# A fused attention and expert kernel: PSUM banks in strict turn, early weights decoded in another order, part of the routing moved to GpSimd

## The chip, the core and the metric

The kernel runs on one core of a Trainium2 chip. Five engines work side by side, each through its own queue of instructions in order: TensorE (PE, with its weight loads as PEld) multiplies matrices into PSUM; VectorE (DVE), ScalarE (ACT) and GpSimd (POOL) work elementwise; SyncE (SP) issues most transfers. They wait for each other through semaphores. The metric is the device time of one execution in microseconds; the time of a kernel is the median of its runs.

## What is computed

Attention with capped scores, a gated product of two linear maps, and a layer of eight experts that sends each token to one of them. All values are float32.

```python
def _attn_ref(q, k, v, cap):                     # 2 x 12 heads, 448 tokens, 64 wide
    scores = cap * np.tanh(scale * q @ k.T / cap)
    attn = softmax(scores)                       # with 1e-9 added to the sum
    return attn @ v

def _moe_ref(x, w_a, w_b, w_out):                # 896 x 768, inner width 1536
    return (x @ w_a) * (x @ w_b) @ w_out

def _moe2_ref(x, w_gate, w1, w2):                # 8 experts, 768 -> 1024 -> 768
    logits = x @ w_gate
    expert_idx = np.argmax(logits, axis=1)
    gate_w = softmax(logits)[expert_idx]
    out[mask_e] = gate_w * (np.maximum(x[mask_e] @ w1[e], 0) @ w2[e])
```

(`q @ k.T` and the softmaxes are abbreviated here; the weights of the product come as 64-bit floats and are decoded on the chip.)

## The kernel before

The instructions stand in each queue in the order in which the code below writes them; no scheduler moves them.

**Attention** (`attention`, L150) walks over 12 pairs of heads. For each pair n, TensorE makes the scores of four chunks of keys (`ps_s`, L100), ScalarE takes Tanh (L104) and for two chunks together Exp (L106) into `e`, and GpSimd adds the two chunks of each half into `u` (L112, the *fold*). VectorE adds the two halves (L115). TensorE multiplies `e` with v (`ps_o`, L125) and, from `u` and a matrix of ones, makes the sums (`ps_sm`, L131). VectorE then takes the reciprocal `r` (L139), multiplies `xf` (L140) and splits that into a high and a low part `xh`, `xl` (L142, L143). One iteration holds the scores of pair n, the product with v of pair n-1, and the sums and the norm of pair n-2. Ahead of the scores VectorE scales the queries of each pair by 1/(8 cap) (`attn_prep`, L91), two pairs ahead. Transfers of `qk` and `v` run through SP's queue, between those of the first raw weights.

In the first two iterations VectorE also decodes the first column blocks of `w_a` and `w_b` (`b1_decode`, L260; `early` puts all of it on VectorE): raw words to float (L253 to L258), high part `wh` (L242), low part `wl` (L268). Before all this `attn_flag` (L59) tests whether |cap| exceeds 40; only then does another path for attention run (`attn_general`).

**PSUM.** Four one-bank tiles carry the tag `p1`, and two two-bank tiles the tag `s2`. A new tile of a tag takes a bank that is free by the pool's record, and its first writer waits for the last reader of the tile before.

**The product** (`b1_products`, L274) computes both linear maps over 12 column blocks, each matmul in three parts (high by high, high by low, low by high). **The output** (`b2_tile`, L492) then makes seven tiles of 128 tokens in `ps_y` (tag `s2`, so two at a time); after each, ScalarE copies the tile to a `row` in SBUF (L508), and `gate_steps` (L545) finds the expert of each token: for tiles 0, 1, 2, 4 and 5 eight VectorE products with a gate column each (`jk`, L569), for tiles 3 and 6 matmuls. `route_steps` (L606) ranks the tokens of a group by expert (tiles 0 to 3 are group 0, tiles 4 to 6 group 1): `ranks`, `totals`, `sizes`, `bases`, `blocks`, `past`, `meta`, `ranked`, `places`, `onehot`, `lists`. The steps of group 1, with what is left of the gate, are a list `todo`; `pop` (L471) writes the next of them into the code of an expert block, seven times in a block.

**The experts** (`d_block`, L845): block s gathers 128 rows by an indirect transfer on GpSimd, loads the weights of its expert, splits them into high parts (ScalarE, L794) and low parts (VectorE, L797: `w1l`, `w2l`), and runs two layers. Between the layers TensorE transposes each half of the hidden values; ScalarE writes `hth`, VectorE the low part `htl` (L823), and the second layer (L842, L843) takes both. Ten blocks are executed here.

Of the kernel before, what the change touches and what calls it, by code (L numbers as in the profile page):

```python
# [23 lines left out]
CP, NCH = 112, 4  # L24
# [13 lines left out]
class Kernel:  # L38
# [20 lines left out]
    def attn_flag(self):  # L59

        nc, cp, cap = self.nc, self.const, self.cap1
        ab = cp.tile([1, 2], F32, name="capabs")
        big = cp.tile([1, 1], I32, name="big")
        nc.vector.tensor_scalar(ab[:, 0:1], cap, -1.0, None, op0=ALU.mult)
        nc.vector.tensor_tensor(ab[:, 1:2], cap, ab[:, 0:1], op=ALU.max)
        nc.vector.tensor_scalar(big, ab[:, 1:2], CAP_DIRECT, None, op0=ALU.is_gt)
        self.bigv = nc.values_load(big[0:1, 0:1], min_val=0, max_val=1)
# [25 lines left out]
    def attn_scores(self, n, c):  # L93

        nc = self.nc
        qk = self.ld[n][0]
        ps = self.ps.tile([128, 2, 512], F32, name="ps_s", tag="s2", bufs=2)
        for j in range(2):
            r = slice(64 * j, 64 * j + 64)
            nc.tensor.matmul(ps[:CP, j, :S], qk[r, 1, c * CP : (c + 1) * CP], qk[r, 0], start=True, stop=True)  # L100
        if c == 0:
            self.e[n] = self.awork.tile([CP, NCH, 2, S], F32, name="e", bufs=2)
        e = self.e[n]
        nc.scalar.activation(e[:, c], ps[:CP, :, :S], AF.Tanh)  # L104
        if c % 2:
            nc.scalar.activation(e[:, c - 1 : c + 1], e[:, c - 1 : c + 1], AF.Exp, scale=self.cap[:CP])  # L106
# [43 lines left out]
    def attention(self):  # L150
# [3 lines left out]
        for n in range(npair):  # L154
            self.attn_load(n + RING - 1)
            self.attn_scores(n, 0)
            self.attn_scores(n, 1)
            if n > 0:
                self.attn_pv(n - 1, 0, 1)
            self.attn_fold(n, 0)  # L160
            if n > 1:
                self.attn_sums(n - 2)
                self.attn_norm(n - 2)
            self.attn_prep(n + 2)
            if n < 2:
                self.b1_decode(0, n, early=True)
            self.attn_scores(n, 2)
            self.attn_scores(n, 3)
            if n > 0:
                self.attn_pv(n - 1, 2, 3)  # L170
            self.attn_fold(n, 1)
        self.attn_pv(npair - 1, 0, 1)
# [4 lines left out]
    def attn_general(self):  # L177
# [10 lines left out]
        with self.tc.If(self.bigv > 0, label="general"):  # L188
            sc = self.attn_scale()
            for b, hp in ((b, hp) for b in range(B) for hp in range(NP)):  # L190
# [3 lines left out]
                po = self.p1("ps_go")  # L194
                for j in range(2):
                    rows = slice(64 * j, 64 * j + 64)
                    et = [tile_of(f"ge{i}", [CP, 2, S]) for i in range(2)]
                    for c in range(NCH):
                        cs = slice(c * CP, (c + 1) * CP)
                        ps, pt = self.p1("ps_gs"), self.p1("ps_gt")  # L200
# [105 lines left out]
    def run(self):  # L306
# [24 lines left out]
        self.raw, self.w = {}, {}  # L331
# [17 lines left out]
        self.attn_prep(0)  # L349
# [161 lines left out]
    def p1(self, name, dt=F32):  # L511
        return self.ps.tile([128, 512], dt, name=name, tag="p1", bufs=4)
# [32 lines left out]
    def gate_steps(self, i, xr, py):  # L545
# [19 lines left out]
        def product(e):  # L565
            if "lg" not in st:
# [3 lines left out]
                jk, py[:, :DM], 1.0, self.wgb[e], op0=ALU.mult, op1=ALU.mult, accum_out=st["lg"][:, e : e + 1],  # L570
# [35 lines left out]
    def route_steps(self, g):  # L606
        nc, tw, n = self.nc, self.tw, GT[g]
        st = {}

        def T(shape, name, dt=F32):  # L610
# [12 lines left out]
        def totals():  # L623
            rk, tt = st["rk"], st["tt"]
            for t in range(1, n):
                nc.vector.tensor_tensor(rk[:, t], rk[:, t], tt[:, t - 1], op=ALU.add)
                nc.vector.tensor_tensor(tt[:, t], tt[:, t], tt[:, t - 1], op=ALU.add)
# [54 lines left out]
        def ranked():  # L682
# [3 lines left out]
            nc.vector.tensor_tensor(pr[:, 0, :n], rk[:, :n], self.oh[g], op=ALU.mult)  # L686
            nc.vector.tensor_tensor(
# [16 lines left out]
        def onehot(t):  # L704
            rp = st["rp"]
            nc.vector.tensor_scalar(st["a"][:, t], self.iota, rp[:, 0, t : t + 1], None, op0=ALU.is_equal)
            tk = GT[0] * g + t
            nc.vector.tensor_scalar(
# [136 lines left out]
    def d_block(self, s):  # L845
# [18 lines left out]
        self.pop()  # L864
        self.d_split2(6)
        ha = self.d_ht(0, ha)
        self.pop()
# [17 lines left out]
        if more:  # L885
            self.d_xt(s + 1, 1)()
            self.d_split1(4, 5)
        self.d_w2(hb, 6, 7)
# [62 lines left out]
```

## Time and profile before

| | |
|---|---|
| median of 3 runs (lowest to highest) | 589.39 us (588.01 to 590.59) |
| the profiled execution | 586.97 us |
| its span, first to last instruction | 585.2 us |
| mean granted TensorE clock | 0.988 |
| busy: PE, DVE, ACT, POOL | 554.0, 478.9, 335.6, 92.4 us |

Attention fills the stretch up to about 112 us, the product the one up to 289 and the output up to 384 us; the expert blocks follow. TensorE is busy for 95% of the span. A time in a row of the timeline is that of the start, then the duration; in square brackets stands how long the engine was idle just before and what released it. A wait of TensorE is what a shorter time can be won from, as far as nothing else becomes late in its place. The granted clock is 1.00 at 2.4 GHz and 0.50 at 1.2 GHz.

### The profile page before, as it was taken

To read this page: it belongs to the slowest core of one execution; us is meant where nothing else is said; L and a number is where in the kernel's file an instruction comes from. 1 tells how busy PE (TensorE), PEld (TensorE's weight loads), DVE (VectorE), ACT (ScalarE), POOL (GpSimd) and SP (SyncE) were. 2 spreads that over 40 slices of the span, in tenths; PEclk is the share of its full clock that TensorE was granted. 3 is DMA by queue.
4 is the path that set the end of the run, shared out by engine and by line. 5 is a ranking of instruction groups with operands and counts; after the bars stand their busy time and mean duration, and the time that the engine had idled before them with its cause. 6 is when DMAs were issued, how large, how long until landed. Compare 5 with 4: busy or idle time off the path is not lost. (4 is left out here: it accounts for less than half of the span.)

```text
span 585.2 us, 8722 instructions
## 1 busy us (share of the span) xinstructions
PE 554.0 (95%) x2835; PEld 432.4 (74%) x2835; DVE 478.9 (82%) x757; ACT 335.6 (57%) x423; POOL 92.4 (16%) x64
## 2 busy tenths in 40 slices
PE   4799999899999999999999999899989999999994
PEld 1222333499999999999988888778868888888883
DVE  1699999988887777777578848887998998988984
ACT  3958998424333333333451121476877789888893
POOL 0645555300000000000000000501020011110110
PEclk9989999999999999999999999999999999999998
DMA  5972200045545444410061006686110499200110
GB/s 175 336 227 95 63 1 0 1 165 203 173 164 176 153 171 158 172 47 39 2 201 43 28 27 238 207 333 228 57 54 28 170 345 387 104 15 28 56 55 34
DMA packets 21344, 75.51 MB, mean 129 GB/s; under 512 B 3553, under 2 KB 3553, under 8 KB 21282
## 3 DMA queue, kind: packets, MB, share of 16 engines
q1 hardware_dynamic: 19458, 67.68, 33.0%
q0 software_dynamic: 1680, 7.10, 3.6%
q8 instruction: 27, 0.44, 0.3%
q14 instruction: 35, 0.29, 0.1%
q10 hardware_dynamic: 144, 0.00, 0.0%
HBM read 118.80 MB, written 6.70 MB: 214 GB/s over the span
## 5 line engine op out<-in xcount | busy, mean ns | idle before, releaser
L284 PE MATMUL ps_ab<-xh,wh 128*128 128x448 f32 x288 | 105.1, 365 | 0.0
L286 PE MATMUL ps_ab<-xh,wl 128*128 128x448 f32 x288 | 105.0, 364 | 0.0
L285 PE MATMUL ps_ab<-xl,wh 128*128 128x448 f32 x288 | 105.0, 364 | 0.0
L797 DVE TENSOR_TENSOR w1l<-r,w1h 128x1024 fp32r<-128x1024 f32 x63 | 74.2, 1220 | 8.8 <-ACT w1h L794 8.8
L797 DVE TENSOR_TENSOR w2l<-r,w2h 128x768 fp32r<-128x768 f32 x80 | 72.4, 952 | 2.8 <-ACT w2h L794 1.9
L244 ACT ACTIVATE wh<-wf 128x768 fp32r<-128x768 f32 x22 | 18.6, 846 | 86.4 <-DVE wf L258 86.4
L794 ACT ACTIVATE w1h<-r 128x1024 fp32r<-128x1024 f32 x66 | 66.2, 1052 | 2.1 <-PE ps_y L500 2.1
L499 PE MATMUL ps_y<-woh,hs 128*128 128x512 f32 x168 | 64.6, 404 | 2.1 <-DVE jk L569 2.1
L112 POOL TENSOR_TENSOR u<-e 112x896 f32<-112x896 f32 x24 | 54.7, 2279 | 54.1 <-ACT e L106 51.4
L794 ACT ACTIVATE w2h<-r 128x768 fp32r<-128x768 f32 x80 | 61.8, 838 | 0.0
L284 PEld LDWEIGHTS ps_ab<-xh,wh 128*128 128x128 f32 x288 | 54.1, 188 | 5.6 <-issue 1.4
L285 PEld LDWEIGHTS ps_ab<-xl,wh 128*128 128x128 f32 x288 | 54.1, 188 | 4.1
L286 PEld LDWEIGHTS ps_ab<-xh,wl 128*128 128x128 f32 x288 | 54.0, 187 | 4.1
L100 PE MATMUL ps_s<-qk 64*112 64x448 f32 x192 | 46.7, 611 | 9.3 <-DVE qk L91 8.6
L104 ACT ACTIVATE e<-ps_s 112x896 f32<-112x896 f32 x48 | 41.4, 909 | 21.7 <-PE ps_s L100 21.6
L500 PE MATMUL ps_y<-woh,hs 128*128 128x256 f32 x168 | 47.1, 281 | 0.0
L100 PEld LDWEIGHTS ps_s<-qk 64*112 64x112 f32 x192 | 16.4, 187 | 38.4 <-issue 14.3
L106 ACT ACTIVATE e<-e,cap 112x1792 f32<-112x1792 f32 x24 | 42.9, 1789 | 0.8
L125 PE MATMUL ps_o<-e,v 112*64 112x448 f32 x192 | 41.3, 552 | 0.0
L569 DVE SCALAR_TENSOR_TENSOR jk<-ps_y,wgb 128x768 f32<-128x768 f32 x40 | 38.3, 957 | 3.6 <-PE ps_ix L716 1.3
L832 PE MATMUL ps_w<-w1h,xht 128*128 128x512 f32 x120 | 40.3, 403 | 0.0
L832 PE MATMUL ps_w<-w1l,xht 128*128 128x512 f32 x120 | 39.6, 397 | 0.0
(154 smaller groups left out, 1069.2 us busy)
## 6 DMA issues: line engine op xcount, KB each, us to landing
r<-w SPq DMA_DIRECT2D x66, 512.0 KB
r<-w SPq DMA_DIRECT2D x88, 384.0 KB
raw_wa<-wa SPq DMA_DIRECT2D x12, 768.0 KB
raw_wb<-wb SPq DMA_DIRECT2D x12, 768.0 KB
raw_wo<-wo SPq DMA_DIRECT2D x12, 768.0 KB
qk<-qk SPq DMA_DIRECT2D x12, 448.0 KB
wgb<-wgt SPq DMA_DIRECT2D x8, 384.0 KB
x1g<-row SPq DMA_DIRECT2D x7, 386.0 KB
```

The lines of the kernel that those rows point to most:

```text
L100: nc.tensor.matmul(ps[:CP, j, :S], qk[r, 1, c * CP : (c + 1) * CP], qk[r, 0], start=True, stop=True)
L104: nc.scalar.activation(e[:, c], ps[:CP, :, :S], AF.Tanh)
L106: nc.scalar.activation(e[:, c - 1 : c + 1], e[:, c - 1 : c + 1], AF.Exp, scale=self.cap[:CP])
L112: self.nc.gpsimd.tensor_tensor(u, e[:, 2 * half], e[:, 2 * half + 1], op=ALU.add)
L284: nc.tensor.matmul(o, wh[:, k], xh, start=k == 0, stop=False)
L285: nc.tensor.matmul(o, wh[:, k], xl, start=False, stop=False)
L286: nc.tensor.matmul(o, wl[:, k], xh, start=False, stop=k == KC - 1)
L499: nc.tensor.matmul(ps[:, 0:512], hs[:, hh, k], w[:, 0:512], start=st, stop=sp)
L500: nc.tensor.matmul(ps[:, 512:768], hs[:, hh, k], w[:, 512:768], start=st, stop=sp)
L794: self.nc.scalar.activation(hl[0], raw, AF.Copy)
L797: (engine or self.nc.vector).tensor_tensor(hl[1], raw, self.f(hl[0]), op=ALU.subtract)
L832: self.nc.tensor.matmul(self.pw1[half], a[:, k], w[:, cs], start=k == 0 and i == 0, stop=k == KC - 1 and i == 2)
```

## The change

1. `p1` gives its four banks in strict turn (a tag for each bank) in place of one tag with four buffers.
2. Pair 0 isn't scaled by VectorE; its Tanh takes the scale. The decode of the first block of `w_a` stands ahead of the scaling of pair 2, that of `w_b` at the end of iteration 0, behind the fold.
3. `attn_flag` is one instruction: cap times cap, compared with 40 squared.
4. The `jk` products of tile 4 read the row copy in SBUF, not `ps_y`.
5. For group 1, `totals`, the products of `ranked` and the one-hots run on GpSimd.
6. In blocks 0 to 3, `htl` of the first half stands ahead of the split of `w2` chunk 6. The pop between the chunks 5 and 6 is dropped, and one is added behind the last split of `w1`, so the steps of group 1 move by a place or so.

```diff
-        ab = cp.tile([1, 2], F32, name="capabs")
-        nc.vector.tensor_scalar(ab[:, 0:1], cap, -1.0, None, op0=ALU.mult)
-        nc.vector.tensor_tensor(ab[:, 1:2], cap, ab[:, 0:1], op=ALU.max)
-        nc.vector.tensor_scalar(big, ab[:, 1:2], CAP_DIRECT, None, op0=ALU.is_gt)
+        nc.vector.tensor_scalar(big, cap, cap, CAP_DIRECT**2, op0=ALU.mult, op1=ALU.is_gt)
...
-        nc.scalar.activation(e[:, c], ps[:CP, :, :S], AF.Tanh)
+        nc.scalar.activation(e[:, c], ps[:CP, :, :S], AF.Tanh, **({} if n else {"scale": self.sc[:CP]}))
...
+            if n == 0:
+                self.b1_decode(0, 0, early=True)
             self.attn_prep(n + 2)
-            if n < 2:
-                self.b1_decode(0, n, early=True)
...
             self.attn_fold(n, 1)
+            if n == 0:
+                self.b1_decode(0, 1, early=True)
...
-        self.attn_prep(0)
         self.attn_prep(1)
...
-    def p1(self, name, dt=F32):
-        return self.ps.tile([128, 512], dt, name=name, tag="p1", bufs=4)
+    def p1(self, name, dt=F32, at=None):
+        if at is None:
+            at = self.turn = (self.turn + 1) % 4
+        return self.ps.tile([128, 512], dt, name=name, tag=f"p1{at}")
...
-                jk, py[:, :DM], 1.0, self.wgb[e], op0=ALU.mult, op1=ALU.mult, accum_out=st["lg"][:, e : e + 1],
+                jk, xr[:, :DM] if i == 4 else py[:, :DM], 1.0, self.wgb[e], op0=ALU.mult, op1=ALU.mult, accum_out=st["lg"][:, e : e + 1],
...
+        eng = nc.gpsimd if g else nc.vector
...
-                nc.vector.tensor_tensor(rk[:, t], rk[:, t], tt[:, t - 1], op=ALU.add)
+                eng.tensor_tensor(rk[:, t], rk[:, t], tt[:, t - 1], op=ALU.add)
...
         self.d_split2(4, 5)
-        self.pop()
-        self.d_split2(6)
+        routing = s < GT[0]
+        if not routing:
+            self.d_split2(6)
         ha = self.d_ht(0, ha)
+        if routing:
+            self.d_split2(6)
         self.pop()
...
             self.d_split1(4, 5)
+        self.pop()
         self.d_w2(hb, 6, 7)
```

The same replacement of `nc.vector` by `eng` stands in `ranked` (two products) and `onehot` (two instructions for each of three tiles). The other path for attention only gets fixed banks.

On VectorE, the opening of attention before (the first row stands for the scaling of pairs 0, 1 and 2; `raw_wa`, `raw_wb` are the raw weights, `u` the fold's add):

```order
L91 TENSOR_SCALAR qk<-qk,sc 128x448 x3
L253 TENSOR_SCALAR wf<-raw_wa 128x768
L256 TENSOR_SCALAR dc<-raw_wa 128x768
L257 SCALAR_TENSOR_TENSOR wf<-wf,k_78,dc 128x768
L258 SCALAR_TENSOR_TENSOR wf<-raw_wa,ksign,wf 128x768
L242 CAST wh<-wf 128x768
L268 TENSOR_TENSOR wl<-wf,wh 128x768
L115 TENSOR_TENSOR u_2333<-u_2333,u_2311 112x896
L91 TENSOR_SCALAR qk<-qk,sc 128x448
L253 TENSOR_SCALAR wf<-raw_wb 128x768
```

And after, from the scaling of pair 1:

```order
L88 TENSOR_SCALAR qk<-qk,sc 128x448
L252 TENSOR_SCALAR wf<-raw_wa 128x768
L255 TENSOR_SCALAR dc<-raw_wa 128x768
L256 SCALAR_TENSOR_TENSOR wf<-wf,k_78,dc 128x768
L257 SCALAR_TENSOR_TENSOR wf<-raw_wa,ksign,wf 128x768
L241 CAST wh<-wf 128x768
L267 TENSOR_TENSOR wl<-wf,wh 128x768
L88 TENSOR_SCALAR qk<-qk,sc 128x448
L112 TENSOR_TENSOR u_2329<-u_2329,u_2307 112x896
L252 TENSOR_SCALAR wf<-raw_wb 128x768
L255 TENSOR_SCALAR dc<-raw_wb 128x768
```

The first decode now follows the scaling of pair 1 at once; that of pair 2 stands behind it, and the second decode ahead of the scaling of pair 3.

On VectorE, block 2 before, around `htl` of the first half (`rt_ri`, `rt_rp` belong to the places, `rt_a`, `rt_b` to the one-hots; `w2l` from `r_6` is that of chunk 6):

```order
L797 TENSOR_TENSOR w2l_5228<-r_5_5162,w2h_5227 128x768
L695 CAST rt_ri<-rt_rr 128x3
L696 TENSOR_SCALAR rt_ri<-rt_ri 128x3
L697 TENSOR_SCALAR rt_ri<-rt_ri 128x3
L698 CAST rt_rp<-rt_ri 128x2x3
L699 TENSOR_TENSOR rt_rp<-rt_rp,rt_rr 128x3
L797 TENSOR_TENSOR w2l_5230<-r_6_5163,w2h_5229 128x768
L823 TENSOR_TENSOR htl<-ps_ht,hth 128x512
L706 TENSOR_SCALAR rt_a<-iota,rt_rp 128x128
L708 TENSOR_SCALAR rt_b<-iota,rt_rp,tok 128x22
```

And after:

```order
L800 TENSOR_TENSOR w2l_5224<-r_5_5158,w2h_5223 128x768
L826 TENSOR_TENSOR htl<-ps_ht,hth 128x512
L800 TENSOR_TENSOR w2l_5226<-r_6_5159,w2h_5225 128x768
L698 CAST rt_ri<-rt_rr 128x3
L699 TENSOR_SCALAR rt_ri<-rt_ri 128x3
L700 TENSOR_SCALAR rt_ri<-rt_ri 128x3
L701 CAST rt_rp<-rt_ri 128x2x3
L702 TENSOR_TENSOR rt_rp<-rt_rp,rt_rr 128x3
L800 TENSOR_TENSOR w2l_5228<-r_7_5160,w2h_5227 128x768
L800 TENSOR_TENSOR w1l_5206<-r_0_4339,w1h_5205 128x1024
```

`htl` has moved ahead of the places and of chunk 6, and the one-hots are gone from VectorE's queue.

On GpSimd after, the blocks 1 to 3 (before, only the gathers `xg` and the stores `out` stood there):

```order
L765 DMA xg_5019<-x1g,idc_131 128x772
L629 TENSOR_TENSOR rt_rk<-rt_rk,rt_tt 128x8
L630 TENSOR_TENSOR rt_tt<-rt_tt 128x8
L629 TENSOR_TENSOR rt_rk<-rt_rk,rt_tt 128x8
L630 TENSOR_TENSOR rt_tt<-rt_tt 128x8
L899 DMA out<-y,idx_129 896x768
L765 DMA xg_5285<-x1g,idc_131 128x772
L689 TENSOR_TENSOR rt_pr<-rt_rk,oh_128 128x24
L690 TENSOR_TENSOR rt_pr<-oh_128,rt_base 128x24
L709 TENSOR_SCALAR rt_a<-iota,rt_rp 128x128
L711 TENSOR_SCALAR rt_b<-iota,rt_rp,tok 128x22
L709 TENSOR_SCALAR rt_a<-iota,rt_rp 128x128
```

Totals, products and one-hots stand there in that order, between and behind the transfers.

## Rows read from the trace of the kernel before

**Rows 1.** TensorE's waits, 0 to 112 us: total, times, longest

```profile
PE ps_sm L131 <- DVE u L115: 3.9, 1, 3.9
PE ps_sm L131 <- DVE r L139: 2.7, 6, 1.7
```

**Rows 2.** TensorE's waits, 382 to 425 us and 425 to 460 us

```profile
PE ps_w L842 <- DVE htl L823: 0.9, 1, 0.9
...
PE ps_w L842 <- DVE htl L823: 3.0, 2, 2.8
```

**Rows 3.** Stretches: length, busy PE, PEld, DVE, ACT, POOL, then clock, DMA share, GB/s

```profile
45.00:60.00 15.00, 14.72 (x72) 4.59 (x68) 14.79 (x13) 13.22 (x13) 9.04 (x4) 1.00 0.28 93
...
112.00:340.00 228.00, 228.00 (x1165) 207.02 (x1162) 180.53 (x324) 77.23 (x111) 0.40 (x5) 1.00 0.35 122
...
367.00:371.00 4.00, 1.94 (x12) 1.46 (x11) 3.79 (x14) 0.30 (x2) 1.24 (x2) 1.00 0.33 99
...
438.00:441.00 3.00, 3.00 (x12) 2.61 (x12) 3.00 (x7) 0.93 (x2) 0.00 (x0) 0.50 0.00 0
```

**Rows 4.** Timeline, opening of attention, VectorE: start, duration, engine, line, operation, tiles

```profile
2.79 0.15 DVE L65 TENSOR_TENSOR capabs<-cap,capabs 1x1 f32<-1x1 f32 x1
...
14.17 0.45 DVE L91 TENSOR_SCALAR qk<-qk,sc 128x448 f32<-128x448 f32 x1 [5.63 <-DMA qk<-qk]
...
19.04 1.52 DVE L91 TENSOR_SCALAR qk<-qk,sc 128x448 f32<-128x448 f32 x1 [4.41 <-DMA qk<-qk]
...
21.53 1.02 DVE L257 SCALAR_TENSOR_TENSOR wf<-wf,k,dc 128x768 int32<-128x768 int32 x1
...
22.59 2.73 DVE L258 SCALAR_TENSOR_TENSOR wf<-raw_wa,ksign,wf 128x768 int32<-128x768 int32 x1
...
37.34 2.95 DVE L139 RECIPROCAL r<-ps_sm 128x448 f32<-128x448 f32 x1
```

**Rows 5.** Timeline, steady attention, VectorE and GpSimd

```profile
45.14 2.94 DVE L139 RECIPROCAL r<-ps_sm 128x448 f32<-128x448 f32 x1
...
49.36 2.42 POOL L112 TENSOR_TENSOR u<-e 112x896 f32<-112x896 f32 x1 [1.34 <-ACT e L106]
49.75 2.28 DVE L91 TENSOR_SCALAR qk<-qk,sc 128x448 f32<-128x448 f32 x1
...
51.95 1.08 DVE L115 TENSOR_TENSOR u<-u,u 112x896 f32<-112x896 f32 x1
...
52.95 2.94 DVE L139 RECIPROCAL r<-ps_sm 128x448 f32<-128x448 f32 x1
...
53.72 2.10 POOL L112 TENSOR_TENSOR u<-e 112x896 f32<-112x896 f32 x1 [1.94 <-ACT e L106]
```

**Rows 6.** Timeline, end of the output stage

```profile
355.20 0.81 ACT L508 ACTIVATE row<-ps_y 128x768 f32<-128x768 f32 x1 [4.50 <-issue]
...
370.22 0.48 PE L499 MATMUL ps_y<-woh,hs 128*128 128x512 f32 x1 [2.06 <-DVE jk L569]
...
382.17 0.69 DVE L785 TENSOR_TENSOR xlt<-ps_xd,xht 128x512 fp32r<-128x512 f32 x1 [2.38 <-ACT xht L784]
```

**Rows 7.** Timeline, expert blocks 0 to 2

```profile
400.89 0.17 DVE L577 COPY lg<-ps_lg 128x8 f32<-128x8 f32 x1 [2.10 <-PE ps_lg L575]
...
415.64 0.19 PEld L842 LDWEIGHTS ps_w<-w2h,htl 128*128 128x128 f32 x1 [0.43 <-DVE htl L823]
...
416.63 0.16 DVE L627 TENSOR_TENSOR rt_tt<-rt_tt 128x8 f32<-128x8 f32 x1
...
434.44 0.16 DVE L695 CAST rt_ri<-rt_rr 128x3 int32<-128x3 f32 x1
...
435.36 0.96 DVE L797 TENSOR_TENSOR w2l<-r,w2h 128x768 fp32r<-128x768 f32 x1
...
436.97 0.51 PE L842 MATMUL ps_w<-w2h,htl 128*128 128x512 f32 x1 [2.76 <-DVE htl L823]
...
448.89 1.27 POOL L891 DMA_INDIRECT out<-y,idx  x1 [19.41 <-ACT y L890]
```

More of the change, by code (lines that the diff above doesn't have):

```diff
@@ L193, in attn_general @@
                 nc.sync.dma_start(v, self.io["v"][b, hp])
-                po = self.p1("ps_go")
+                po = self.p1("ps_go", at=0)
                 for j in range(2):
@@ L199, in attn_general @@
                         cs = slice(c * CP, (c + 1) * CP)
-                        ps, pt = self.p1("ps_gs"), self.p1("ps_gt")
+                        ps, pt = self.p1("ps_gs", at=1 + c % 2), self.p1("ps_gt", at=3)
                         nc.tensor.matmul(ps[:CP, :S], qk[rows, 0, cs], qk[rows, 1], start=True, stop=True)
@@ L330, in run @@
         self.gx = tc.dram_tile((B, 2, 128, KC, S), F32, name="gx")
-        self.raw, self.w = {}, {}
+        self.raw, self.w, self.turn = {}, {}, 0
         self.xg, self.xt = {}, {}
@@ L625, in totals @@
             for t in range(1, n):
-                nc.vector.tensor_tensor(rk[:, t], rk[:, t], tt[:, t - 1], op=ALU.add)
-                nc.vector.tensor_tensor(tt[:, t], tt[:, t], tt[:, t - 1], op=ALU.add)
+                eng.tensor_tensor(rk[:, t], rk[:, t], tt[:, t - 1], op=ALU.add)
+                eng.tensor_tensor(tt[:, t], tt[:, t], tt[:, t - 1], op=ALU.add)
         def sizes():
@@ L685, in ranked @@
             pr, rr = T([2, 4, NE], "pr"), T([2, 4], "rr")
-            nc.vector.tensor_tensor(pr[:, 0, :n], rk[:, :n], self.oh[g], op=ALU.mult)
-            nc.vector.tensor_tensor(
+            eng.tensor_tensor(pr[:, 0, :n], rk[:, :n], self.oh[g], op=ALU.mult)
+            eng.tensor_tensor(
                 pr[:, 1, :n], self.oh[g], base.unsqueeze(1).to_broadcast([128, n, NE]), op=ALU.mult
@@ L705, in onehot @@
             rp = st["rp"]
-            nc.vector.tensor_scalar(st["a"][:, t], self.iota, rp[:, 0, t : t + 1], None, op0=ALU.is_equal)
+            eng.tensor_scalar(st["a"][:, t], self.iota, rp[:, 0, t : t + 1], None, op0=ALU.is_equal)
             tk = GT[0] * g + t
-            nc.vector.tensor_scalar(
+            eng.tensor_scalar(
                 st["b"][:, t], self.iota[:, :NSP], rp[:, 1, t : t + 1], self.tok[:, tk : tk + 1],
```

## The prediction

> **What bounds the kernel now.** I read first the list of TensorE's waits, stretch by stretch, because only an engine that never waits sets the time. From 112 to 340 us the list is empty and TensorE is busy for 228.00 of 228.00 us [rows 3]; from 460 us to the end it is empty again. What the change could give there is nothing, and it touches nothing there. So the whole effect has to come out of three places, and I read each in the timeline. (A) Attention: TensorE waits 3.9 us once for a folded sum `u` and 2.7 us in six places for the reciprocal `r`, both made by VectorE [rows 1]. VectorE is busy for 14.79 of 15 us while attention runs steadily [rows 3], so there it is VectorE that sets the pace: one pair costs it 52.95 - 45.14 = 7.81 us [rows 5]. (B) The output product: its last tile waits 2.06 us for the products `jk` of tile 4 [rows 6]. (C) The expert blocks 0 to 3: waits for `htl` of 0.9 us in block 0 and 3.0 us in two places later [rows 2], of which 2.76 us stand at 436.97 in block 2 [rows 7]; a last one, of 0.43 us in block 1 at 415.64, is too short for the list [rows 7].
>
> **A: the opening and the banks.** Before, VectorE sits idle for 4.41 us until pair 2's queries land at 19.04, and only then decodes the first weights [rows 4]. After, the same work stands between the scaling of pair 1 and the first reciprocal, but the first decode goes ahead of that wait, and the second goes behind the first fold. The weights of that decode were asked for ahead of pair 1's queries, which are there at 14.17, so the decode can start then. That closes 4.41 us. The flag loses two instructions of some 0.17 us each from start to start (one is shown at 2.79), which stand before the branch and so before those loads: 0.35 us. Sum 4.76.
>
> What it costs shows in the same rows. A VectorE instruction that reads only SBUF and meets a GpSimd fold takes about 1.7 to 1.8 us longer: 2.73 against 1.02 for two like steps of the decode [rows 4], and 2.28 against 0.45 for the same scaling, with a fold at 49.36 beside it [rows 5, 4]. The Trainium skill states why ("SBUF — State Buffer", "Who interferes with whom": VectorE with two SBUF inputs, or in a two-port mode, and a GpSimd instruction that reads SBUF hold one port pair by turns, for a whole instruction each); the rows agree, though it names no price. The fold of pair 0's first half met an idle VectorE; now it meets a decode: +1.75. The next one cost only 1.07 (scaling 1.52 against 0.45 [rows 4]); now it meets a longer instruction: +0.7. So 4.76 - 2.45 = 2.3 us; I take the first reciprocal 2.0 us earlier than 37.34 [rows 4]. If one fold more collides before it, 0.3 is left.
>
> Pair 0's scaling moves into its Tanh: 0.45 us (the price of the one at 14.17 [rows 4]) go from the way to the first matmul, but TensorE is not late there, so I cost it at nothing; the cover is the wait for pair 1's queries.
>
> The strict turn of the four banks moves a wait, no instruction. Before, the sums of pair n took the bank of the sums of pair n-1, so TensorE stood until that reciprocal was read (six waits, 2.7 us [rows 1]). After, the output of pair n takes the bank of pair n-2's output and waits for VectorE's `xf`, the instruction behind the reciprocal, one iteration later; pv, sums and the next scores are queued behind it. In the steady part VectorE is full, so TensorE only waits elsewhere: nothing gained, and nothing lost as long as VectorE's 7.81 us hold. What the opening gives is then carried to the end of attention: **A = -2.0**. The bound on the good side is 4.41, if the folds collide no more than before; on the bad side I take one pair's collision, +1.5, for new ones in the steady part.
>
> **B: tile 4's gate from SBUF.** The wait of 2.06 us at 370.22 is for a bank that eight `jk` instructions read; after, they read the row copy, which ScalarE has made at 355.20 (0.81 us), and the bank is free twelve us too early to matter [rows 6]. What is late next: the first expert input is split by VectorE at 382.17, after 2.38 us of idle time [rows 6], so VectorE can come forward by most of this. Two SBUF inputs may cost each `jk` up to 0.13 us, which is how far the decode's like step (1.02 [rows 4]) lies from theirs, 1 us in all; that eats idle time first. **B = -2.0**, between -2.06 and -1.0.
>
> **C: routing of the second group.** In blocks 0 to 3 `htl` now stands ahead of `w2l` of chunk 6, worth 0.96 us [rows 7]. Block 0's wait of 0.9 goes, and block 1's 0.43. In block 2 VectorE has no pause between 410 and 441 us, so what leaves its queue ahead of `htl` counts in full: `w2l` 0.96; the five place instructions, from 434.44 to 435.36, 0.92, now behind `htl`; the four running totals at 0.14 each from start to start (one at 416.63), 0.55; two products, 0.25 [rows 7]. That is 2.7 us. VectorE also starts the blocks about 1.5 us earlier (B), and the 2.10 us that it lost at 400.89 waiting for a transpose [rows 7] may go, since that step is popped later. TensorE comes 2.06 + 0.9 + 0.43 = 3.4 us earlier to the spot. So 436.9 - 2.7 - 1.5 - (0 to 2.1) against 434.2 - 3.4: a wait of 0 to 1.9, where it was 2.76; I take 1.2. After the 2.76 us the granted clock was 0.50 for all of 438 to 441 [rows 3], its lower level (1.2 GHz); 3.0 us at half speed lose 1.5, and I add 0.2 for the edges: 1.7. After the 2.06 us at 370.22 it stayed at 1.00 [rows 3]. So a wait of 1.2 should not lower it. Behind that, `w2l` 6 and the places now stand ahead of the second half's `htl`, and TensorE comes to it early and fast: a new wait of 0.6 to 1.6, taken as 1.0. Sum: -0.9 - 0.4 - 1.5 - 1.7 + 1.0 = **C = -3.5**, between -1.5 (below) and -5.5 (no wait in block 2).
>
> GpSimd gets twelve small instructions. Its queue in these blocks holds only a gather and a store each, with 19.41 us idle ahead of the store at 448.89 [rows 7]. The totals stand behind block 2's gather, the products behind block 3's; one-hots come last, and TensorE asks for them only in block 3. No row prices them on GpSimd; a fold of 896 columns takes 2.42 [rows 5], so by its length one of 128 columns takes 0.35 or so, and the small ones not under VectorE's 0.14. I take 0.3, 3.6 us in all, well inside the idle time; both ends leave it there.
>
> **Sum.** -2.0 - 2.0 - 3.5 = -7.5. The profiled execution takes 586.97 us for a span of 585.2, and lies 2.4 below the median of 589.39; I expect an execution like it at 579.5 and a median of **581.9**.
>
> **The rivals.**
> - *GpSimd gives it back.* Each moved instruction reads SBUF, and VectorE does little but subtractions of two SBUF inputs there. If each of the twelve holds VectorE for its 0.3 us, 3.6 come back, more than totals and products (0.8) and the six one-hots saved; the clock falls again in block 2 and C is -1.5: 583.9. For it speak the collisions in A; against it, that only the six of totals and products stand ahead of the critical `htl`. The Trainium skill speaks against such moves ("Perfetto Trace Analysis", "Optimizing Scalar/DVE Operations": the two engines share a read port, so offloading between them might not help). By it the sum would be that of this rival; the trace of before has no small GpSimd instruction among the blocks, and so leaves it open. 0.20.
> - *The opening gives nothing.* A sixth collision, or weights that land later than I read, leave A between 0 and -0.3; with B and C as above -5.5 to -5.8, and with a worse tail -4: about 584. 0.15.
> - *The opening gives all.* If folds slip between PSUM-fed instructions, A is -4.4: 579.5. 0.13.
> - *Slower: the folds meet the fold's add in every pair.* GpSimd's first fold of a pair starts at 53.72, 1.77 us after the add at 51.95 has started [rows 5]. TensorE no longer stands for the reciprocal, so scores, Exp and that fold can run ahead. From the point where the fold starts before the add, each pair loses 2.28 - 0.45 = 1.83 [rows 5, 4], on top of the collision that it has. Five pairs outweigh the -7.5; nine give +16.5 and 598.4. Against it: `e` has two buffers, and VectorE's add is what lets GpSimd go on. 0.08.
> - *The turn changes nothing.* The matmuls keep their order, so if `xf` comes as late for TensorE as the reciprocal did, only the place of the wait differs. That is inside my forecast, since I give the turn nothing.
>
> **Chances.** The forecast as it stands 0.42; with the rivals above 0.98; 0.02 for what I don't see. A measurement of this kernel can tell about 0.5%, 2.9 us, from no change, so faster means under 586.4: the forecast, the upper opening, most of the GpSimd rival and of the weak opening, together 0.80. Within 0.5%: the rest of these two, 0.12. Slower 0.08. The range runs from 577 (the good bounds of A and half of C's) to 587 (two of the weak cases together); it leaves out the slower rival and the ends.
>
> **What would show it.** First reciprocal near 35.3, and the product stage some 2 us earlier; no wait for `jk`; `htl` of blocks 0 and 1 without a wait; in block 2 a wait under 2 us and a clock of 1.00 behind it. Wrong would be: scaling and fold's add both over 2 us in each pair; VectorE's `w1l` and `w2l` lengthened beside GpSimd's one-hots; a clock of 0.50 near 435.

## The result, and the profile after

The changed kernel takes 579.72 us (median of 4 runs, 578.74 to 580.21), the kernel before 589.53 us beside it. The ratio is 0.9833, with a 95% interval of 0.9808 to 0.9859: 9.8 us less, where 7.5 were forecast. The profiled execution has a span of 577.0 us, 8.2 less than the 585.2 of before. The sign, the size and the three places were forecast rightly; of the three terms, two came out much as worked out and one, the opening of attention, came by another way. The ratios leave out executions over 1.5% above the fastest of the same kernel, which below concerns two of the twelve of e1_turn, at 922.08 and 1112.86 us.

TensorE's waits of the changed kernel (engine, line, waited for, total, times, longest), from 0 to 112 us and from 425 to 460 us; from 112 to 425 us the list is empty:

```profile
PE ps_s L97 <- PEq L187: 8.1, 1, 8.1
PE ps_s L97 <- issue: 4.1, 2, 3.8
PE ps_s L97 <- DVE qk L88: 2.9, 1, 2.9
PE ps_o L122 <- ACT e L103: 1.3, 1, 1.3
...
PE ps_w L845 <- DVE htl L826: 1.4, 2, 1.1
```

The first line is the time up to the first matmul, 8.6 us in the kernel before. The waits for `u` and `r` [rows 1] are gone. In their place stand 2.9 us for the scaled queries of pair 1, 3.8 us that the profile gives no releaser ("issue"), and 1.3 us for `e` near the end of attention. The 3.8 us end when VectorE has scaled the queries of pair 3, as the rows below show (34.36 and 2.26 us). The wait for `jk` is gone, and of those for `htl` [rows 2] 1.4 us are left, 1.1 in one place.

Where the 8.2 us come from is read from the first instructions of each stage, in us from the start of the span:

| first instruction | before | after | gain so far |
|---|---|---|---|
| product stage (`ps_ab`) | 112.75 | 111.24 | 1.5 |
| output stage (`ps_y`) | 288.68 | 287.17 | 1.5 |
| experts (`ps_w`) | 383.64 | 379.24 | 4.4 |
| store of block 1 | 425.94 | 420.37 | 5.6 |
| store of block 2 | 448.89 | 440.67 | 8.2 |
| store of block 9 | 577.88 | 569.82 | 8.1 |

The opening of attention after, VectorE and one row of TensorE (start, duration, engine, line, operation, tiles; in brackets the idle time before and its releaser):

```profile
7.75 0.16 DVE L69 RECIPROCAL sc<-cap 128x1 f32<-128x1 f32 x1 [4.96 <-DVEq L187]
...
14.67 2.02 DVE L88 TENSOR_SCALAR qk<-qk,sc 128x448 f32<-128x448 f32 x1 [6.57 <-DMA qk<-qk]
...
18.71 2.73 DVE L257 SCALAR_TENSOR_TENSOR wf<-raw_wa,ksign,wf 128x768 int32<-128x768 int32 x1
...
23.02 2.29 DVE L88 TENSOR_SCALAR qk<-qk,sc 128x448 f32<-128x448 f32 x1
...
27.28 2.74 DVE L256 SCALAR_TENSOR_TENSOR wf<-wf,k,dc 128x768 int32<-128x768 int32 x1
...
31.11 2.34 DVE L241 CAST wh<-wf 128x768 fp32r<-128x768 f32 x1
...
34.36 2.26 DVE L88 TENSOR_SCALAR qk<-qk,sc 128x448 f32<-128x448 f32 x1
...
36.73 3.07 PE L97 MATMUL ps_s<-qk 64*112 64x448 f32 x8 [3.80 <-issue]
37.55 2.94 DVE L136 RECIPROCAL r<-ps_sm 128x448 f32<-128x448 f32 x1
```

Between 14.67 and the reciprocal VectorE has no pause left, as intended; but six of its instructions, those of over 2 us, meet a fold and take 1.6 to 1.8 us more each. The reciprocal starts at 37.55, where it started at 37.34 before [rows 4].

The first pairs after the reciprocal, and the steady part (VectorE and GpSimd):

```profile
41.61 0.63 DVE L140 TENSOR_TENSOR xl<-xf,xh 128x448 fp32r<-128x448 f32 x1
...
43.52 2.95 DVE L136 RECIPROCAL r<-ps_sm 128x448 f32<-128x448 f32 x1
...
47.15 2.09 POOL L109 TENSOR_TENSOR u<-e 112x896 f32<-112x896 f32 x1 [1.60 <-DVE xf L137]
47.16 2.33 DVE L139 CAST xh<-xf 128x448 fp32r<-128x448 f32 x1
...
50.07 0.45 DVE L88 TENSOR_SCALAR qk<-qk,sc 128x448 f32<-128x448 f32 x1
50.43 1.08 DVE L112 TENSOR_TENSOR u<-u,u 112x896 f32<-112x896 f32 x1
50.59 2.88 POOL L109 TENSOR_TENSOR u<-e 112x896 f32<-112x896 f32 x1 [1.34 <-ACT e L103]
```

The scaling takes 0.45 us, not the 2.28 of before [rows 5], and the cast of `xh` meets a fold in its place. The add at 50.43 starts 0.16 us ahead of the second fold, and it is the fold that waits (2.88 us in place of 2.09). From one reciprocal to the next, attention now goes like this. The first pair takes 5.97 us (37.55 to 43.52), where it took 7.80: no fold runs beside its `xl` (0.63 us), where one did in the kernel before:

```profile
41.41 2.44 DVE L143 TENSOR_TENSOR xl<-xf,xh 128x448 fp32r<-128x448 f32 x1
```

The seven pairs behind it, up to 96.54, take 7.57 us each, where a pair took 7.81. The last three, up to the last reciprocal at 116.11, take 19.57 us together, where they took 17.78.

Block 2 after (TensorE, VectorE, GpSimd), and two stretches (length, busy PE, PEld, DVE, ACT, POOL, clock, DMA share, GB/s):

```profile
429.76 0.50 PE L845 MATMUL ps_w<-w2h,htl 128*128 128x512 f32 x1 [1.14 <-DVE htl L826]
...
435.37 0.51 PE L845 MATMUL ps_w<-w2h,htl 128*128 128x512 f32 x1 [0.23 <-DVE htl L826]
```

```profile
412.96 1.18 POOL L630 TENSOR_TENSOR rt_tt<-rt_tt 128x8 f32<-128x8 f32 x1
414.22 0.20 POOL L629 TENSOR_TENSOR rt_rk<-rt_rk,rt_tt 128x8 f32<-128x8 f32 x1
...
435.53 2.29 POOL L711 TENSOR_SCALAR rt_b<-iota,rt_rp,tok 128x22 fp32r<-128x22 f32 x1
...
438.39 0.45 POOL L711 TENSOR_SCALAR rt_b<-iota,rt_rp,tok 128x22 fp32r<-128x22 f32 x1
...
432.27 2.44 DVE L800 TENSOR_TENSOR w1l<-r,w1h 128x1024 fp32r<-128x1024 f32 x2
```

```profile
430.00:436.00 6.00, 5.77 (x35) 4.90 (x35) 5.86 (x11) 4.09 (x6) 4.63 (x4) 1.00 0.00 1
```

The wait in block 2 is 1.14 us, where it was 2.76 [rows 7], and the clock stays at 1.00 behind it, where it fell to 0.50 [rows 3]. GpSimd's small instructions last from 0.20 to 2.29 us, by what VectorE does beside them; two `w1l` together take 2.44 us beside them at 432.27, and 2.34 to 2.36 elsewhere, with GpSimd idle or not.

### The profile page after: what moved, and what is told of

The parts are those of the page before. It is cut to its first block, busy times and chain, and to the rows that moved or that the text cites. A ratio compares the mean times of both kernels' runs of the same rounds, so it can differ in the third digit from the quotient of the medians.

```text
span 577.0 us, 8727 instructions
## 1 busy us (share of the span) xinstructions
PE 550.4 (95%) x2835; PEld 432.8 (75%) x2835; DVE 478.5 (83%) x742; ACT 335.2 (58%) x423; POOL 107.9 (19%) x76
## 4 chain that ended last, share of the span: by engine, by line
PE 54%; issue 19%; DVE 17%; DMA 6%; ACT 2%; POOL 1%; POOLq 0%; SPq 0%; DVEq 0%; ACTq 0%
PE ps_y L497 10%; PE ps_ab L283 10%; PE ps_ab L284 10%; PE ps_ab L285 10%; PE ps_y L498 5%; DMA out<-y,idx 5%; DVE r L136 4%; PE ps_w L835 3%; DVE xh L139 2%; DVE u L112 2%; PE ps_w L845 1%; DVE qk L88 1%; DVE w2l L800 1%; DMA qk<-qk 1%; DVE xf L137 1%
## 5 line engine op out<-in xcount | busy, mean ns | idle before, releaser
L109 POOL TENSOR_TENSOR u<-e 112x896 f32<-112x896 f32 x24 | 59.4, 2476 | 48.5 <-ACT e L103 39.0
L101 ACT ACTIVATE e<-ps_s 112x896 f32<-112x896 f32 x44 | 38.0, 910 | 12.1 <-PE ps_s L97 12.1
L267 DVE TENSOR_TENSOR wl<-wf,wh 128x768 fp32r<-128x768 f32 x24 | 23.0, 959 | 20.2 <-ACT wh L243 20.1
L835 PE MATMUL ps_w<-w1h,xlt 128*128 128x512 f32 x120 | 39.3, 395 | 0.0
```

The lines of the kernel that those rows point to most:

```text
L109: self.nc.gpsimd.tensor_tensor(u, e[:, 2 * half], e[:, 2 * half + 1], op=ALU.add)
L835: self.nc.tensor.matmul(self.pw1[half], a[:, k], w[:, cs], start=k == 0 and i == 0, stop=k == KC - 1 and i == 2)
```

## The experiments

Two theories stood against each other after the first look. By the prediction, the opening brings the first reciprocal forward and the turn of the banks does nothing. By the trace after, the reciprocal is no earlier, and the pairs follow each other faster. The first four kernels each make one part of the change alone; a time in us beside a ratio is the ratio times 588.3, the median of before on that chip (588.6 and 589.4 in the later two groups).

### e1_turn: the turn of the banks alone

```diff
...
-        return self.ps.tile([128, 512], dt, name=name, tag="p1", bufs=4)
+        if at is None:
+            at = self.turn = (self.turn + 1) % 4
+        return self.ps.tile([128, 512], dt, name=name, tag=f"p1{at}")
```

> The kernel before with the four banks in strict turn and nothing else. What the prediction said: the turn only moves TensorE's wait, 0 us; a pair keeps VectorE's 7.81 us and the product stage starts at 112.7. The theory formed on the trace after (there the first reciprocal is no earlier, 37.55, but pairs follow each other every 7.50 us on average): the turn alone shortens the pair, because TensorE's scores and so GpSimd's folds run ahead and meet other VectorE instructions; the product stage starts 1.5 to 2.5 us earlier (10 pairs by 0.2 to 0.3), and the time is 1.5 to 2.5 us shorter. A first reciprocal near 37.3 under both.

Ratio 1.001 (0.9988 to 1.0031). Some pairs do become shorter, but at a price; TensorE's waits, 0 to 112 us:

```profile
...
PE ps_sm L131 <- DVE u L115: 3.9, 1, 3.9
PE ps_o L125 <- DVE xf L140: 2.2, 2, 1.8
PE ps_s L100 <- ACT e L104: 1.9, 2, 1.6
```

The seven pairs behind the second reciprocal take 52.98 us (45.39 to 98.37), where they took 54.69. The last three take 19.54, where they took 17.78, and the last reciprocal comes at 117.91, 0.3 later than before; the product stage begins at 113.06. So the end of attention eats what the shorter pairs give. The prediction's value for the turn (nothing) holds, though its reason does not: the wait is moved, and the period changes as well.

### e2_opening: the opening alone

```diff
+            if n == 0:
+                self.b1_decode(0, 0, early=True)
             self.attn_prep(n + 2)
-            if n < 2:
-                self.b1_decode(0, n, early=True)
...
+            if n == 0:
+                self.b1_decode(0, 1, early=True)
...
-        self.attn_prep(0)
```

(with the Tanh of pair 0 and the flag as in the change)

> The kernel before with the other order of the first decoding, pair 0 scaled in its Tanh and the flag in one instruction; banks as before. What the prediction said: the first reciprocal at 35.3, the product stage 2.0 us earlier. The theory formed on the trace after: the earlier folds collide with more of VectorE's work and the first reciprocal stays near 37.5; the period stays at 7.81, the product stage starts within 0.5 us of 112.75 and the time is within 1 us of before.

Ratio 0.9974 (0.9955 to 0.9992): 1.5 us less. Both theories missed. The first reciprocal is at 37.49, no earlier, against the prediction; but the product stage begins at 109.05, 3.7 us earlier, against the other. VectorE and TensorE over 50 us of the steady part of this kernel, then one pair of it:

```profile
60.00:110.00 50.00, 50.00 (x245) 17.47 (x242) 49.28 (x40) 44.19 (x39) 32.49 (x14) 1.00 0.06 19
```

```profile
61.98 2.10 POOL L109 TENSOR_TENSOR u<-e 112x896 f32<-112x896 f32 x1 [1.12 <-ACT e L103]
62.34 1.72 PE L122 MATMUL ps_o<-e,v 112*64 112x448 f32 x8
62.47 1.86 DVE L139 CAST xh<-xf 128x448 fp32r<-128x448 f32 x1
```

TensorE never waits for 50 us, and a pair takes 7.44; over the same 50 us it is busy for 47.75 in the kernel before. Of the 2.25 us missing there, 1.35 belong to one wait, up to 110.34, and the rest is some 0.15 in each pair, for `r`. VectorE is as full as before (49.28 of 50). So a full VectorE did not mean that VectorE sets the pace: part of its busy time is a cast that stands until a fold has ended (62.47 to 64.33, with the fold ending at 64.08), and that part gives way. The cast loses 1.47 us by it (1.86 against the 0.39 of one that meets no fold), where the scaling lost 1.83 before; the difference, 0.36, is that of the pairs. What sets 7.81 in the kernel before is, as I read these rows, the round of waits: the sums wait for the reciprocal of the pair before [rows 1], the scores behind them feed the fold, the fold holds the scaling (2.28), and that delays the next reciprocal. The opening, by its new order, starts the steady part with TensorE far enough ahead that the sums never meet the reciprocal. No run tests this round by itself.

Of the 3.7 us, 2.6 are left at the output stage (286.10 against 288.68): the first product takes 1.1 us more here. TensorE waits 0.3 us there for products of VectorE, which is late with the next decode. The last reciprocal of attention is a better mark than the first matmul of the product: it comes at 115.17, 2.4 us earlier than before (117.61), and in each of the thirteen profiles the output stage begins 170.9 to 171.1 us behind it. What in the product holds to it is not read from these rows. And behind the wait of 2.06 us for `jk` the clock fell in this run, as it did not before ([rows 3], and 1.00 from 372 to 376 us as well):

```profile
368.00:372.00 4.00, 4.00 (x15) 3.43 (x16) 3.38 (x12) 2.30 (x5) 0.05 (x1) 0.57 0.42 118
```

### e3_jk: tile 4 from SBUF alone

```diff
-                jk, py[:, :DM], 1.0, self.wgb[e], op0=ALU.mult, op1=ALU.mult, accum_out=st["lg"][:, e : e + 1],
+                jk, xr[:, :DM] if i == 4 else py[:, :DM], 1.0, self.wgb[e], op0=ALU.mult, op1=ALU.mult, accum_out=st["lg"][:, e : e + 1],
```

> The kernel before with tile 4's gate products read from the row copy in SBUF. If the step stands by itself: no wait for jk, the first matmul of the experts 2.06 us earlier, and 2.0 us less in all. Rival: without the changes in the blocks VectorE does not come forward as far as TensorE, the wait for htl in block 2 grows from 2.76 to over 3.2 and 0.5 to 1.5 us of the gain is lost there, so 0.6 to 1.6 us less in all. Both theories expect each jk at 0.96 us as before; the bound of the prediction was 1.09.

Ratio 0.9944 (0.9922 to 0.9966): 3.3 us less, more than either. The experts begin 2.28 us earlier (381.36). Then, in block 2 (TensorE, and a stretch):

```profile
434.68 0.50 PE L842 MATMUL ps_w<-w2h,htl 128*128 128x512 f32 x1 [2.72 <-DVE htl L823]
```

```profile
434.00:438.00 4.00, 3.32 (x20) 2.99 (x21) 4.00 (x11) 1.18 (x2) 0.00 (x0) 1.00 0.00 0
```

The wait is as long as before (2.72 against 2.76 [rows 7]), VectorE having come forward as far as TensorE, against the rival. But the clock stays at 1.00, where it was 0.50 [rows 3]. From the first matmul of the experts to the store of block 2 it takes 63.64 us, where it took 65.25 with the same waits, so the clock is worth 1.6 us there and makes the rest of the gain in this profile (3.89 at the store of block 2). The profiled execution is 2.2 us faster than the median of its kernel (582.94 against 585.12), so the clock need not have stayed in all of them. `jk` takes 0.96 us from SBUF as from PSUM, so the bound of 0.13 more is void:

```profile
360.94 0.96 DVE L570 SCALAR_TENSOR_TENSOR jk<-row,wgb 128x768 f32<-128x768 f32 x1
```

(that row is from the changed kernel).

### e4_blocks: the expert blocks alone

```diff
+        eng = nc.gpsimd if g else nc.vector
...
-        self.pop()
-        self.d_split2(6)
+        if not routing:
+            self.d_split2(6)
         ha = self.d_ht(0, ha)
+        if routing:
+            self.d_split2(6)
...
             self.d_split1(4, 5)
+        self.pop()
```

> The kernel before with the changes in the expert blocks alone: second group's routing on GpSimd, htl ahead of w2l 6, the moved pop. By the prediction 3.5 us less: waits for htl of 0.9 and 0.4 gone, that of block 2 at 1 to 2 us, a clock of 1.00 behind it (1.7 of the 3.5). Rival, GpSimd gives it back: wait in block 2 over 2 us, a clock of 0.50 behind it, 1.5 us less. The trace after shows GpSimd's instructions of 0.2 us stretched up to 2.3 while VectorE's keep their length; under the theory that VectorE, which has its next instruction ready, always goes first, VectorE's w1l stay at 1.22 us here too.

Ratio 0.993 (0.9905 to 0.9955): 4.1 us less, where the prediction has 3.5. The waits in blocks 0 and 1 are gone, that in block 2 is 1.2 us, and the clock behind it is 1.00. The four parts alone make +0.6 - 1.5 - 3.3 - 4.1 = -8.3, and all together make -9.8; within the intervals they add up, though the clock in block 2, 1.6 us, can stand in two of the parts (e3_jk and e4_blocks).

### e5_no_gpsimd: the changed kernel with the routing on VectorE

```diff
-        eng = nc.gpsimd if g else nc.vector
...
-                eng.tensor_tensor(rk[:, t], rk[:, t], tt[:, t - 1], op=ALU.add)
+                nc.vector.tensor_tensor(rk[:, t], rk[:, t], tt[:, t - 1], op=ALU.add)
...
```

(and the same replacement in all the instructions that had moved)

> The changed kernel with the second group's routing left on VectorE; the moved pop and htl ahead of w2l 6 stay. If the move to GpSimd relieves VectorE by what leaves its queue ahead of block 2's htl (totals 0.55, products 0.25): that wait grows from 1.1 to about 1.9, and behind it the six one-hots (1.2) stand ahead of the second half's htl, whose wait grows from 0.2 to about 1.4; 1.5 to 2 us longer than the changed kernel, more by some 1.5 if the clock falls again. If GpSimd gives back what it saves: same time within 0.5 us.

Ratio 0.9891 (0.9873 to 0.991), against 0.9833 for the changed kernel: 3.4 us lost. Of these, 1.1 stand in the opening, where this kernel is the same (product stage at 112.35), and are no effect of the edit. In the blocks TensorE waits 1.85 us at `htl` and the clock falls; the second wait that was expected, at the other half's `htl`, does not come:

```profile
431.86 0.50 PE L843 MATMUL ps_w<-w2h,htl 128*128 128x512 f32 x1 [1.85 <-DVE htl L824]
```

```profile
434.00:438.00 4.00, 4.00 (x20) 3.58 (x20) 4.00 (x8) 2.49 (x3) 0.00 (x0) 0.69 0.00 0
```

From the first matmul of the experts to the store of block 2 it takes 63.17 us, 61.43 in the changed kernel and 65.25 in the kernel before. So the other order is worth 2.1 us there and the move to GpSimd 1.7, the clock included, and the rival that GpSimd gives it back has fallen. The reason is on GpSimd's side, in the rows of block 2 after: its instructions are the ones that stand.

### e6_no_turn: the changed kernel without the turn

```diff
...
-        return self.ps.tile([128, 512], dt, name=name, tag=f"p1{at}")
+        return self.ps.tile([128, 512], dt, name=name, tag="p1", bufs=4)
```

> The changed kernel with the four banks given out as before. By the prediction (the turn only moves a wait) no difference from the changed kernel. By the theory from the two runs before (product stage at 109.05 with the opening alone, at 111.24 with opening and turn): the turn makes the product with v of pair n wait for xf of pair n-2, costs 0.07 us a pair and 1.3 at the last; without it the product stage starts at 109.0 to 109.3 and the span is 1 to 2 us shorter than 577.0, some of the 2.2 being lost in the product stage, where VectorE is then late with the decode.

Ratio 0.9836 (0.9818 to 0.9854): the same as the changed kernel. The product stage begins at 110.21, 1.0 earlier, and the output stage at 287.24, as late as with the turn (287.17). The theory that the turn costs 1 to 2 us has fallen as a statement on the time: the first matmul of the product moves, but the last reciprocal does not come earlier (116.32 against 116.11).

### e7_tanh4 and e8_tanh_all: scaling in the Tanh

The new waits of the changed kernel before 40 us are for queries that VectorE has to scale. The Tanh can take the scale, as that of pair 0 does: in e7 for pairs 0 to 3, in e8 for all. Both build on e6_no_turn.

Of e7_tanh4:

```diff
-        nc.scalar.activation(e[:, c], ps[:CP, :, :S], AF.Tanh, **({} if n else {"scale": self.sc[:CP]}))
+        nc.scalar.activation(e[:, c], ps[:CP, :, :S], AF.Tanh, **({} if n > 3 else {"scale": self.sc[:CP]}))
...
-            self.attn_prep(n + 2)
+            if n > 1:
+                self.attn_prep(n + 2)
...
-        self.attn_prep(1)
```

Of e8_tanh_all:

```diff
-        nc.scalar.activation(e[:, c], ps[:CP, :, :S], AF.Tanh, **({} if n else {"scale": self.sc[:CP]}))
+        nc.scalar.activation(e[:, c], ps[:CP, :, :S], AF.Tanh, scale=self.sc[:CP])
...
-            self.attn_prep(n + 2)
...
-        self.attn_prep(1)
```

> The kernel of e6_no_turn, with pairs 0 to 3 scaled in their Tanh and without their scaling on VectorE. In the opening of the changed kernel TensorE waits 2.9 us for the scaling of pair 1 and 3.8 for that of pair 3, and has a clock of 0.50 for 3 us behind it. Theory (these waits set the start of the steady part): TensorE's waits before 40 us fall from 7 to under 3, the reciprocal is 3 to 5 us earlier, and the product stage starts 2 to 5 us earlier. Rival (VectorE's decode, with its collisions, sets it): TensorE waits as long at the sums instead, product stage within 1 us of e6_no_turn. Tanh with a scale from SBUF takes 1.01 against 0.92, 0.09 more, four times in each of four pairs.

> The kernel of e6_no_turn, all 12 pairs scaled in Tanh and no scaling on VectorE. Opening as in e7_tanh4. In the steady part ScalarE gets 0.36 us more a pair, 6.9 to 7.3 of a pair's 7.44 on TensorE. If TensorE still paces: same as e7_tanh4 within 0.5. If ScalarE, which also has waits, becomes the bound: pairs at 7.6 or more, and 1 to 3 us longer than e7_tanh4.

Ratios 0.9777 (0.9756 to 0.9799) and 0.9758 (0.9741 to 0.9775): 576.15 and 574.15 us, both faster than the changed kernel. TensorE's waits before 40 us in e7_tanh4:

```profile
PE ps_sm L128 <- DVE r L136: 4.6, 1, 4.6
PE ps_s L97 <- DMA qk<-qk: 1.9, 1, 1.9
```

The first reciprocal comes only 1.0 earlier than in e6_no_turn (36.39), and the product stage at 108.97. So half of each theory holds: the waits for scaled queries are gone, and one for the reciprocal, behind VectorE's decodes, has taken their place. In e8_tanh_all the pairs keep 7.45 us (95.47 to 102.92, for one), so ScalarE, with 0.36 more a pair, is not the bound. Nor is VectorE: it has lost the scaling (0.45 a pair), and the pair does not become shorter than the 7.44 of e2_opening. The profiled executions of e6_no_turn, e7_tanh4 and e8_tanh_all are the slowest of their kernels (580.75, 578.04 and 578.08 us against medians of 579.10, 576.15 and 574.15), so what stands in them can lie some microseconds later than in a usual execution.

### e9_spread: the second decode in single instructions

```diff
-            if n == 0:
-                self.b1_decode(0, 1, early=True)
+            if n == 1:
+                steps = self.b1_decode_steps(0, 1)
+            if 1 < n < 8:
+                steps.pop(0)()
```

(`b1_decode_steps` returns the six instructions of the decode as a list; built on e8_tanh_all.)

> The kernel of e8_tanh_all with the second decode in six single instructions, one at the end of each iteration 2 to 7, in the place that the scaling had. In e8_tanh_all TensorE's one long wait before 40 us is 4.6 us for the first reciprocal, which VectorE reaches at 36.9 behind the two decodes. Theory (that wait is worth what it lasts): first reciprocal at 28 to 31, the wait of 4.6 under 1, product stage at 104 to 107 in place of 109.1, 2 to 5 us less than e8_tanh_all. Rival (VectorE, at 14.8 of 15 us busy, is the bound as soon as it gets one instruction more a pair): pairs at 7.7 us or more in iterations 2 to 7, product stage within 1 us of 109.1.

Ratio 0.9696 (0.9672 to 0.972): 570.94 us, 3% under the kernel before and 1.4% under the changed kernel. First reciprocal, first matmul of the product, and two stretches:

```profile
28.16 2.95 DVE L136 RECIPROCAL r<-ps_sm 128x448 f32<-128x448 f32 x1
...
100.60 0.47 PE L304 MATMUL ps_ab<-xh,wh 128*128 128x448 f32 x1
```

```profile
36.00:42.00 6.00, 6.00 (x32) 2.10 (x30) 5.90 (x5) 5.93 (x6) 4.48 (x2) 1.00 0.94 267
...
60.00:100.00 40.00, 40.00 (x198) 13.78 (x196) 39.41 (x30) 38.28 (x32) 26.02 (x12) 1.00 0.03 7
```

The reciprocal is 8.8 us earlier than in the profile of e8_tanh_all. But that execution was 3.9 us slower than its median, and its first decode began at 14.94, when the raw weights had landed, where it began at 12.81 here. Against e10_tanh_turn (below), which began it at 12.50, the reciprocal is 4.3 us earlier, and the time 4.5 us shorter. In attention no wait for VectorE is left, and the clock stays at 1.00 from 15 us on. The product stage begins at 100.60, 10.6 us before that of the changed kernel and earlier than the 104 to 107 that were expected; the last reciprocal, at 106.89, is 9.2 us before that of the changed kernel. VectorE takes the additional instructions, one a pair from 35.85 on, without TensorE's waiting: the full VectorE gives way here too.

### e10_tanh_turn and after_again

e10_tanh_turn is e8_tanh_all with the three lines of e1_turn; after_again is the changed kernel, unedited.

> The kernel of e8_tanh_all with the four banks in strict turn. By the prediction's reading (the turn only moves a wait) no difference to e8_tanh_all. By the theory that it costs 1.3 at the last pair and 0.07 a pair: product stage 1 to 2 us later than 109.1. Part of that comes back in the first product, where the kernels without the turn took 14.2 us and those with it 13.0, so the time differs by under 1 us in either case.

> The changed kernel once more, on the same chip as the two others: 577.0 us span and 9.8 us less than before, to set e9_spread and e10_tanh_turn against it directly, and to see how far the opening of one kernel differs from run to run (product stage 111.24 in its first profile).

e10_tanh_turn: 0.9771 (0.9746 to 0.9796), the same as e8_tanh_all. Its first reciprocal is 4.4 us earlier than in the profile of e8_tanh_all:

```profile
32.50 2.94 DVE L136 RECIPROCAL r<-ps_sm 128x448 f32<-128x448 f32 x1
```

Its product stage is earlier too (106.50), not later, so the stage marks of single profiles do not bear out a cost of the turn either. after_again: 0.9831 (0.9804 to 0.9858), a span of 578.4, first reciprocal at 37.13, product stage at 111.62, wait in block 2 of 1.1 at a clock of 1.00. One kernel's opening differs by some 0.4 us between these two profiles, and by 1.1 with e5_no_gpsimd.

## Why the prediction was right, and where it was not

**A, the opening (forecast -2.0, measured -1.5 in the trace).** The size came out by luck; the step behind it failed. The first reciprocal was to come 2.0 us earlier and came 0.2 later. Two terms were off. The flag's 0.35 did not arrive: the branch releases VectorE at 7.75 after and 7.70 before, so something else lets it go. And of the 4.76 the collisions were to take 2.45. Six instructions lengthened by 1.57, 1.71, 1.84, 1.72, 1.78 and 1.81, which is 10.4 us, where four of before (two of them in [rows 4], the others at 25.35 and 31.07) lost 6.2: 4.2 more. Pair 1's queries came 0.5 later as well. That is the second rival, the sixth collision, to the letter: the opening's own gain is nothing. What made attention 1.5 us shorter lies behind that reciprocal: 0.2 us are lost up to it, 1.8 gained in the first pair, 1.7 in the seven pairs behind it, and 1.8 lost in the last three. The first pair gains because no fold meets it: TensorE had stood for pair 3's queries, and GpSimd is idle from 36.4 to 42.65; this and the loss at the end stand nowhere in the prediction, and why the last three are longer is not read from these rows. The 1.7 us are a step that the prediction had excluded, "In the steady part VectorE is full, so TensorE only waits elsewhere: nothing gained". e2_opening shows it wrong: the busy time of an engine that stands for another's instruction is not its work. The clock of the opening had no price either. It fell in both kernels: to 0.58 from 30 to 36 us before, behind the wait of 3.9 us for `u`, and to 0.72 from 36 to 42 us after, behind the one of 3.8.

**The turn (forecast 0).** Three pairs of kernels with and without it differ by nothing that can be measured: e1_turn and before, the changed kernel and e6_no_turn, e10_tanh_turn and e8_tanh_all.

**B, tile 4's gate (forecast -2.0).** Right in the trace: the wait is gone, the experts begin 2.9 us earlier than the output stage's start accounts for, 2.06 of which is the wait, and the rest lies in stretches without waits. It is not a fixed gain: by the same two marks it is 2.4 us in after_again and 1.8 in e6_no_turn. VectorE came forward as read from its 2.38 us of idle time. The bound of 0.13 us for a `jk` was misread, 1.02 lying 0.06 above their 0.96, and was not needed. Alone this part gives 3.3 us, more than the 2.0 given to it; in the profile of e3_jk the surplus is the clock in block 2. That is a term of C that appears here.

**C, the blocks (forecast -3.5, measured -3.8 in the trace).** Right step by step: block 0 and 1 without a wait, 1.14 us in block 2 (forecast 1.2), a clock of 1.00 (1.7), and the new wait at the second half 0.23, where 1.0 was forecast. These terms, with 1.6 for the clock by e3_jk, make 4.3, so 0.5 more than the stage gained; where that stays is not read from the rows. The last term was too dear: I had counted what stands ahead of that `htl` after the change, and not that the six one-hots, which stood there before, have left. From the first matmul of the experts to the store of block 2 it takes 65.2 to 65.3 us in the three profiles of unchanged blocks whose clock fell (before, e1_turn, e2_opening), and 61.3 to 61.4 in all eight with the whole of this part, so C does not hang on one execution.

**The rivals.** GpSimd did not give it back: the move was worth 1.7 us (e5_no_gpsimd). Its twelve instructions were priced at 0.3 us each, 3.6 in all, and last 12.1; free of VectorE they are 0.20 to 0.59. The contention that the rival named is there, but on the other side. The Trainium skill says in "SBUF — State Buffer", "Who interferes with whom", that the order of issue decides who blocks; the trace agrees in part. VectorE, with an instruction always ready, keeps its length (2.44 against 2.35 for two) and GpSimd stands for up to 2 us; but the one-hot at 432.76 stood for 2.21 us, through the second `w1l` too, which by the trace started behind it, at 433.5. The slower rival did not happen, by little: the fold did run ahead, and starts 0.16 us behind the add, not 1.77. By the rival's reckoning each pair would have paid, had it come ahead; no run shows steady pairs of that kind.

**The sum.** -1.5, -2.9 and -3.8 in the trace make 8.2; the timed runs say 9.8, with an interval of 8.3 to 11.3. The forecast of 7.5 stands 0.8 outside that interval on the small side, and the time of 579.72 inside the range of 577 to 587. The profiled execution of before was 2.6 us faster than its median (586.97 against 589.53), and the one of after 1.0 (578.74 against 579.72), which is the difference. The lower end of the range does not follow from its own terms: 581.9 less 2.4 for A and 1 for half of C's is 578.5, not 577; the measured time lies above both.

## What to carry to other kernels

An engine that is busy almost all of the time need not set the pace: look whether some of its instructions are longer than the same ones elsewhere, and ask which engine never waits. A block of work that nobody needs soon (here a decode that is due behind 100 us) belongs in single instructions between those that others wait for, not in front of the first of them; from e8_tanh_all to e9_spread that was worth 0.6%, over a third of what the whole change gave. VectorE and GpSimd delayed each other in both directions here: a VectorE instruction beside a fold lost 1.5 to 1.8 us, a small GpSimd instruction beside VectorE's subtractions up to 2. So a small instruction on the idle engine cost the busy one little (2.44 against 2.35 us), and nobody waited for it.

## What the runs showed that was not expected

- The clock behind a wait does not follow from the length of the wait alone. In block 2 it fell after 2.76 us (before), 2.72 (e1_turn) and 1.85 (e5_no_gpsimd), and stayed at 1.00 after 2.72 (e3_jk). At the output's last tile it stayed at 1.00 after 2.06 us in the kernel before and in e4_blocks, and fell after the same 2.06 in e1_turn and e2_opening. The prediction inferred from one row with 2.06 us that a wait of 1.2 is safe; waits of 1.1 to 1.2 were so in each of the eight profiles with them, but that rule is not shown. What decides stays open, and with it how much of e3_jk's 3.3 us is the clock.
- GpSimd's additions of 128 x 8 take 0.20 us and its comparison of 128 x 128 takes 0.59 us with VectorE out of the way; beside VectorE's subtractions up to 2.3 us.
- Tanh with a scale read from SBUF takes 1.01 us where it takes 0.92 without one.
